# The matrix of one for the transposes: one counting instruction of GpSimd and one comparison, in place of a chain of pieces on VectorE

## Chip, cores and metric

One Trainium2 chip, one core. The time is device microseconds of one launch, the median of the timed runs. In rows of the trace PE is TensorE's matmul, PEld its weight load, DVE is VectorE, ACT ScalarE, POOL GpSimd, SP SyncE, which here does nothing but issue DMAs; a "q" behind the name is the engine's sequencer.

## What is computed

Block-causal attention (8 batches, 8 heads, 576 positions, 64 wide), then a gated feed-forward layer over all 4608 tokens:

```python
scores = q @ k.T / sqrt(64)            # (8, 8, 576, 576)
scores = where(pos_i // 64 >= pos_j // 64, scores, -1e9)
attn = softmax(scores) @ v             # heads side by side: x is (4608, 512)
g = x @ w_gate                         # (512, 1536)
out = (g / (1 + exp(-g)) * (x @ w_val)) @ w_out
```

The float64 weights are turned into pairs of float32 parts on the chip, so each product of the feed-forward layer is three matmuls (L1100 to L1102, L1191 to L1193).

## The kernel before

A planner in the kernel (`in_order`) simulates five engines with costs written by hand and lists all steps in one order; they are issued in that order, so every engine has a fixed queue. The planner's tasks begin behind the lines that the change touches, and neither its costs nor its ranks are touched.

Before the planner's list stands the setup. VectorE sets `ones`, `unseen` and `seen`. GpSimd clears tiles as they are made (the loop over `first_of`: `v` at L260, `ob` at L281, the key columns of `parts` at L234). Then VectorE makes `ident`, a 128x128 matrix with ones on its diagonal, in 13 instructions (L308 to L316): a row 0 to 127 by doubling, each partition's own number by a transpose and three additions, and one comparison.

`ident` is an operand of the transposes on TensorE (L411) that turn q and k of the first two batches. Those feed scores (L437), their maximum (VectorE L702, L705; GpSimd L709, a reduction over partitions), the subtraction (VectorE L733) and the exponential (ScalarE L737). The loads of q come by SyncE (L387), the first eight of k by ScalarE's queue (L387), v by SyncE (L754). In SyncE's queue the first load of `v0` is the third instruction, behind two loads of q; it waits for the GpSimd memset that clears `v0`. Behind it stand the loads of q for the second tile `qk1` and for the second half of `qk0`, and then the loads of the weights (L944).

Of the kernel before, what the change touches and what calls it, by code (L numbers as in the profile page):

```python
# [9 lines left out]
I32 = mybir.dt.int32  # L10
F16 = mybir.dt.float16
AF = mybir.ActivationFunctionType
ALU = mybir.AluOpType
# [5 lines left out]
def kernel(  # L19
# [17 lines left out]
    nc = tc.nc  # L37
# [3 lines left out]
    P = 128  # L41
# [64 lines left out]
    def pool_of(pool, tag, count, shapes=None, init=None, **variants):  # L106

        variants = variants or {"": (shapes, init)}
        kinds[tag] = pool, variants
        slots[tag] = [[None, None] for _ in range(count)]

    def tiles_of(tag, place, variant=""):
        pool, variants = kinds[tag]
        slot = slots[tag][place]
        if slot[0] != variant:
            shapes, init = variants[variant]  # L120
            names = [f"{tag}{place}_{k}" for k in range(len(shapes))]
            slot[:] = variant, [
                x and pool.tile(*x, name=name, tag=name, bufs=1) for x, name in zip(shapes, names)
            ]
            if init:
                init(*slot[1])
        return slot[1]
# [56 lines left out]
    ident = const.tile([P, P], F32, name="ident")  # L184
# [112 lines left out]
    pool_of(psum, "gv", 2, [([P, 2 * XT], F32)])  # L297
    pool_of(psum, "po", 1, [([P, 2, DM], F32)])

    first_of = [("v", ""), ("ob", "signs" if wide else "out"), ("parts", "pair"), ("xhl", ""), ("wo", "raw"), ("hhl", "")]  # L300
    for tag, variant in first_of:
        for place in range(len(slots[tag])):
            tiles_of(tag, place, variant)


    scratch = tiles_of("t", 0)[0]
    count, mine = scratch[:, 0:P], scratch[:, P : P + 32]
    nc.vector.memset(count[:, 0:1], 0.0)  # L308
    for i in range(7):
        n = 2**i  # L310
        nc.vector.tensor_scalar(count[:, n : 2 * n], count[:, 0:n], float(n), None, ALU.add)
    nc.vector.transpose(mine, count[:, 0:32])
    for i in range(1, P // 32):
        rows = slice(32 * i, 32 * (i + 1))
        nc.vector.tensor_scalar(mine[rows, 0:1], mine[rows, 0:1], 32.0 * i, None, ALU.add)
    nc.vector.tensor_scalar(ident, count, mine[:, 0:1], None, ALU.is_equal)  # L316

    x_d = dram.tile([DM, NT], F32, name="x_d")
    s_d = dram.tile([H, NT], F32, name="s_d")
# [1094 lines left out]
```

## Time and profile before

| | |
|---|---|
| median of 3 runs | 1178.03 us (1176.53 to 1178.63) |
| profiled execution | 1175.4 us |
| its span, first to last instruction | 1173.6 us |
| PE busy | 1145.5 us, 98% of the span |
| DVE, ACT, POOL busy | 758.9, 620.4, 325.5 us |

The span is what the trace covers; 1.8 us of the profiled execution lie outside it. A timeline row gives the start, how long it lasted, the engine, line and operation, and in brackets how long the engine sat idle before it and what released it.

### The profile page before, as it was taken

What the parts mean: (1) busy time and instruction counts of PE and PEld (TensorE: products, weight loads), DVE (VectorE), ACT (ScalarE), POOL (GpSimd) and SP (SyncE); (2) the same over time, 40 slices, a digit from 0 to 9 for tenths busy, and PEclk for the clock granted to TensorE, in tenths of its full rate; (3) what the DMA queues carried; (4) which work ended last, traced back from release to release, by engine and by line L of the source; (5) the groups of instructions that cost most, each with busy time, mean ns of one, the idle gap of its engine ahead of it and who ended that gap; (6) DMA issues with size and microseconds to landing.
All of it is one profiled execution on the core that took longest, in us unless ns stands there. A gap on an engine that the chain in (4) does not pass through costs nothing.

```text
span 1173.6 us, 21780 instructions
## 1 busy us (share of the span) xinstructions
PE 1145.5 (98%) x8512; PEld 1024.7 (87%) x8512; DVE 758.9 (65%) x1230; ACT 620.4 (53%) x1114; POOL 325.5 (28%) x139
## 2 busy tenths in 40 slices
PE   5889999999999999999999999999999999999998
PEld 4568778898898989988998899898989899999997
DVE  6988988575887668768575859575767533323222
ACT  6978876546573837465656555555646312212111
POOL 3222100144535251434444334252432500000000
PEclk9989999999999999999999999999999999999999
DMA  8658756766564756656565565655663445444432
GB/s 225 188 151 219 201 187 226 206 178 166 169 148 137 198 164 167 195 166 168 152 188 160 152 177 163 187 146 161 164 202 108 145 148 197 140 167 136 143 134 100
DMA packets 266982, 197.40 MB, mean 168 GB/s; under 512 B 195264, under 2 KB 231376, under 8 KB 266880
## 3 DMA queue, kind: packets, MB, share of 16 engines
q1 hardware_dynamic: 264304, 195.29, 56.9%
q8 instruction: 67, 1.10, 0.4%
q10 hardware_dynamic: 2576, 0.72, 0.3%
q14 instruction: 35, 0.29, 0.1%
HBM read 171.57 MB, written 24.38 MB: 167 GB/s over the span
## 4 chain that ended last, share of the span: by engine, by line
PE 85%; DVE 5%; ACT 4%; DMA 3%; issue 1%; POOL 1%; SPq 1%; ACTq 0%; DVEq 0%; POOLq 0%
PE gv L1100 16%; PE gv L1102 15%; PE gv L1101 15%; PE po L1191 7%; PE po L1193 7%; PE po L1192 7%; PE at L777 7%; PE at L564 6%; DVE sc L733 1%; DVE mx L705 1%; DMA wo<-in_moe_w_val_dram 1%; POOL mx L709 1%; DMA wo<-in_moe_w_out_dram 1%; ACT ob L959 1%; PE at L648 1%
## 5 line engine op out<-in xcount | busy, mean ns | idle before, releaser
L709 POOL PARTITION_ALL_REDUCE mx<-mx x80 | 144.1, 1850 | 408.7 <-issue 135.2
L1100 PE MATMUL gv<-xhl,v_all 128*128 128x256 f32 x864 | 241.8, 280 | 0.8 <-DVE t L1136 0.7
L1102 PE MATMUL gv<-xhl,v_all 128*128 128x256 f32 x864 | 239.7, 277 | 0.0
L1101 PE MATMUL gv<-xhl,v_all 128*128 128x256 f32 x864 | 239.3, 277 | 0.0
L828 POOL PARTITION_ALL_REDUCE mx<-mx x48 | 178.9, 3775 | 201.4 <-DVE mx L705 192.8
L1136 DVE SCALAR_TENSOR_TENSOR t<-t,gv 128x512 f32<-128x512 f32 x108 | 74.0, 685 | 215.4 <-ACT t L1133 215.2
L1100 PEld LDWEIGHTS gv<-xhl,v_all 128*128 128x128 f32 x864 | 162.1, 188 | 4.9 <-issue 2.5
L1101 PEld LDWEIGHTS gv<-xhl,v_all 128*128 128x128 f32 x864 | 162.3, 188 | 0.6
L1102 PEld LDWEIGHTS gv<-xhl,v_all 128*128 128x128 f32 x864 | 162.2, 188 | 0.2
L1133 ACT ACTIVATE t<-gv 128x512 f32<-128x512 f32 x108 | 64.6, 598 | 171.2 <-PE gv L1102 171.1
L1191 PE MATMUL po<-wo,hhl 128*128 128x512 f32 x372 | 147.7, 397 | 0.0
L1192 PE MATMUL po<-wo,hhl 128*128 128x512 f32 x372 | 145.6, 391 | 0.0
L1193 PE MATMUL po<-wo,hhl 128*128 128x512 f32 x372 | 145.1, 390 | 0.2 <-DVE hhl L1149 0.2
L1146 ACT CAST hhl<-t 128x512 fp32r<-128x512 f32 x108 | 67.0, 620 | 132.1 <-DVE t L1141 129.7
L733 DVE TENSOR_TENSOR sc<-sc,mx 128x640 f32<-128x640 f32 (+6 forms) x168 | 122.7, 765 | 11.7 <-POOL mx L709 11.6
L737 ACT ACTIVATE sc<-sc 128x1024 f32<-128x1024 f32 (+3 forms) x104 | 106.0, 1029 | 45.3 <-DVE sc L733 44.9
L1100 PE MATMUL gv<-xhl,g_even 128*128 128x256 f32 x432 | 123.7, 286 | 0.0
L1102 PE MATMUL gv<-xhl,g_even 128*128 128x256 f32 x432 | 122.2, 283 | 0.4 <-DVE g_even L981 0.4
L1101 PE MATMUL gv<-xhl,g_even 128*128 128x256 f32 x432 | 122.1, 283 | 0.0
L1100 PE MATMUL gv<-xhl,g_odd 128*128 128x256 f32 x432 | 120.7, 279 | 0.0
L1101 PE MATMUL gv<-xhl,g_odd 128*128 128x256 f32 x432 | 119.6, 277 | 0.0
L1102 PE MATMUL gv<-xhl,g_odd 128*128 128x256 f32 x432 | 119.6, 277 | 0.0
(171 smaller groups left out, 2368.8 us busy)
## 6 DMA issues: line engine op xcount, KB each, us to landing
wo<-wo_d SPq DMA_DIRECT2D x200, 512.0 KB
out_dram<-ob SPq DMA_DIRECT2D x35, 256.0 KB
v<-in_v_dram SPq DMA_DIRECT2D x64, 128.0 KB
xt<-x_d SPq DMA_DIRECT2D x64, 128.0 KB
rt<-r_d SPq DMA_DIRECT2D x128, 64.0 KB
qk<-in_q_dram SPq DMA_DIRECT2D x112, 72.0 KB
qk<-in_k_dram SPq DMA_DIRECT2D x104, 72.0 KB
x_d<-xu SPq DMA_DIRECT2D x24, 288.0 KB
```

What stands on the lines that cost most here:

```text
L709: nc.gpsimd.partition_all_reduce(m, m, channels=P, reduce_op=bass_isa.ReduceOp.max)
L733: nc.vector.tensor_tensor(piece(c), scores_of(c), m, ALU.subtract)
L737: nc.scalar.activation(x, x, AF.Exp)
L777: nc.tensor.matmul(ps[0][own(x), 1 - i if sums else i, q0 - s0 : s1 - s0], lhsT=ones if sums else vt[0][:, 2 * lane + c, own(x)], rhs=sc[0 ...
L828: nc.gpsimd.partition_all_reduce(m, m, channels=P, reduce_op=bass_isa.ReduceOp.add)
L1100: nc.tensor.matmul(o, lhsT=hi[:, d], rhs=xhi[:, 0:w], start=first, stop=False)
L1101: nc.tensor.matmul(o, lhsT=hi[:, d], rhs=xlo[:, 0:w], start=False, stop=False)
L1102: nc.tensor.matmul(o, lhsT=lo[:, d], rhs=xhi[:, 0:w], start=False, stop=last)
L1136: nc.vector.scalar_tensor_tensor(t[0][:, 0:n], t[0][:, 0:n], 1.0, pg[0][:, 0:n], ALU.add, ALU.mult)
L1191: nc.tensor.matmul(po, lhsT=hi, rhs=whi, start=i + y == 0, stop=False)
L1192: nc.tensor.matmul(po, lhsT=hi, rhs=wlo, start=False, stop=False)
L1193: nc.tensor.matmul(po, lhsT=lo, rhs=whi, start=False, stop=i + y == NFC - 1)
```

## The change

GpSimd's `iota` writes into each element of a scratch tile its column number minus its partition number, as int32; VectorE compares that with 0 and writes `ident`. This stands ahead of the `first_of` loop, so the iota is ahead of GpSimd's memsets, and the scratch tile `t0` is placed in memory ahead of the tiles of that loop.

```diff
+    scratch = tiles_of("t", 0)[0].bitcast(I32)[:, 0:P]
+    nc.gpsimd.iota(scratch, [[1, P]], channel_multiplier=-1)
+    nc.vector.tensor_scalar(ident, scratch, 0, None, ALU.is_equal)
+
     first_of = [("v", ""), ("ob", "signs" if wide else "out"), ("parts", "pair"), ("xhl", ""), ("wo", "raw"), ("hhl", "")]
     for tag, variant in first_of:
         for place in range(len(slots[tag])):
             tiles_of(tag, place, variant)
-
-
-    scratch = tiles_of("t", 0)[0]
-    count, mine = scratch[:, 0:P], scratch[:, P : P + 32]
-    nc.vector.memset(count[:, 0:1], 0.0)
-    for i in range(7):
-        n = 2**i
-        nc.vector.tensor_scalar(count[:, n : 2 * n], count[:, 0:n], float(n), None, ALU.add)
-    nc.vector.transpose(mine, count[:, 0:32])
-    for i in range(1, P // 32):
-        rows = slice(32 * i, 32 * (i + 1))
-        nc.vector.tensor_scalar(mine[rows, 0:1], mine[rows, 0:1], 32.0 * i, None, ALU.add)
-    nc.vector.tensor_scalar(ident, count, mine[:, 0:1], None, ALU.is_equal)
```

GpSimd's queue from the kernel's first instruction, before. The number at a tile's name is its place (`v0`, `v1`) and a running number; DVE_49 and Pool_49 are the semaphores that those engines count up.

```order
L260 MEMSET v0_0_78 128x640
L260 MEMSET v1_0_80 128x640
L281 MEMSET ob0_0_82 128x512
L281 MEMSET ob1_0_84 128x512
L234 MEMSET parts0_1_87 128x64
L234 MEMSET parts1_1_90 128x64
L709 ISA
L709 ISA mx0_0_181<-mx0_0_181 128x256 [waits DVE_49]
```

The same queue now (the lines move up by 8: L701 is what L709 was).

```order
L302 ISA
L302 IOTA t0_0_78 128x128
L260 MEMSET v0_0_81 128x640
L260 MEMSET v1_0_83 128x640
L281 MEMSET ob0_0_85 128x512
L281 MEMSET ob1_0_87 128x512
L234 MEMSET parts0_1_90 128x64
L234 MEMSET parts1_1_93 128x64
L701 ISA
L701 ISA mx0_0_170<-mx0_0_170 128x256 [waits DVE_49]
```

Two instructions came in at the front: the iota, and an ISA instruction without operands ahead of it, of the kind that already stood ahead of the first reduction over partitions and stands there still. All memsets moved behind both.

VectorE's queue before, from the transpose that makes the partitions' numbers to its first step of the planner's list (the doubling rows of L311 ahead of the transpose are not shown).

```order
L312 STREAM_TRANSPOSE t0_0_117<-t0_0_117 128x32
L311 TENSOR_SCALAR t0_0_117<-t0_0_117 128x64 [waits DVE_49]
L315 TENSOR_SCALAR t0_0_117<-t0_0_117 32x1 [waits DVE_49]
L315 TENSOR_SCALAR t0_0_117<-t0_0_117 32x1 x2
L316 TENSOR_SCALAR ident_63<-t0_0_117 128x128 [waits DVE_49]
L702 COPY mx0_0_181<-at0_0_171 128x2x128 [waits PE_49,Activation_49]
```

And now, from its setup memsets on.

```order
L190 MEMSET unseen_66 64x1
L192 MEMSET seen_69 128x1
L303 TENSOR_SCALAR ident_63<-t0_0_78 128x128 [waits Pool_49]
L694 COPY mx0_0_170<-at0_0_160 128x2x128 [waits PE_49,Activation_49]
L697 TENSOR_TENSOR mx0_0_170<-mx0_0_170,at0_0_160 128x2x128
```

Twelve instructions fewer stand there; the comparison that is left waits for GpSimd (Pool_49) in place of VectorE's own chain. SyncE's queue holds the same rows in the same order, its third row among them:

```order
L379 DMA qk0_0_126<-in_q_dram 96x3x64 x2
L746 DMA v0_0_81<-in_v_dram 128x2x64 [waits Pool_49]
L746 DMA v0_0_81<-in_v_dram 128x2x64
L379 DMA qk1_0_134<-in_q_dram 96x3x64 [waits DMAHW1_49]
L379 DMA qk1_0_134<-in_q_dram 96x3x64 [waits DMAHW3_49]
L379 DMA qk1_0_134<-in_q_dram 96x3x64 [waits DMAHW5_49]
L379 DMA qk1_0_134<-in_q_dram 96x3x64 [waits DMAHW7_49]
L379 DMA qk0_0_126<-in_q_dram 96x3x64 [waits DMAHW0_49]
```

Nothing moved here; the wait for Pool_49 is for the second thing that GpSimd finishes in place of the first.

## Rows read from the trace of the kernel before

**Rows 1.** The page: busy us, share of the span, instructions by engine.

```profile
PE 1145.5 (98%) x8512; PEld 1024.7 (87%) x8512; DVE 758.9 (65%) x1230; ACT 620.4 (53%) x1114; POOL 325.5 (28%) x139
```

**Rows 2.** Busy time by stretch: us, busy (instructions) by engine, PEclk, DMA share, GB/s.

```profile
core 0: us, PE busy (x) PEld busy (x) DVE busy (x) ACT busy (x) POOL busy (x), PEclk, DMA share, GB/s
0.00:10.00 10.00, 4.07 (x21) 3.05 (x21) 3.93 (x19) 3.45 (x7) 2.96 (x11) 1.00 0.77 178
...
30.00:40.00 10.00, 7.32 (x71) 5.18 (x67) 9.55 (x22) 9.40 (x18) 2.76 (x2) 1.00 0.66 162
...
60.00:66.10 6.10, 3.72 (x31) 2.47 (x29) 5.92 (x13) 5.00 (x11) 1.50 (x2) 1.00 0.24 52
66.10:72.90 6.80, 5.87 (x28) 3.04 (x30) 6.09 (x12) 3.47 (x8) 0.54 (x1) 0.50 0.75 209
...
100.00:120.00 20.00, 20.00 (x158) 16.81 (x157) 17.42 (x30) 18.16 (x36) 4.33 (x4) 1.00 0.92 262
```

**Rows 3.** Timeline of the first 20 us, engines mixed.

```profile
0.73 1.20 POOL L260 MEMSET v<- 128x640 f32 x2 [0.29 <-POOLq L1397]
...
1.69 0.97 SPq L754 DMA_DIRECT2D v<-in_v_dram  x2
...
2.85 0.23 POOL L234 MEMSET parts<- 128x64 f32 x2
2.98 3.77 SPq L387 DMA_DIRECT2D qk<-in_q_dram  x6
...
4.10 0.28 DVE L316 TENSOR_SCALAR ident<-t 128x128 f32<-128x128 f32 x1
...
4.44 1.22 PE L411 MATMUL gv<-ident,qk 96*128 96x96 f32 x6 [4.44 <-DVE ident L316]
5.37 0.74 ACT L419 ACTIVATE parts<-gv 128x288 f32<-128x288 f32 x2 [2.15 <-DMA qk<-in_k_dram]
...
8.74 0.42 DVE L702 COPY mx<-at 128x256 f32<-128x256 f32 x1 [4.36 <-ACT mx L482]
...
8.78 2.44 PE L411 MATMUL gv<-ident,qk 96*128 96x96 f32 x12 [0.97 <-DMA qk<-in_q_dram]
...
9.59 2.11 POOL L709 PARTITION_ALL_REDUCE mx<-mx  x2 [6.51 <-DVE mx L705]
...
11.73 1.02 DVE L733 TENSOR_TENSOR sc<-at,mx 128x512 f32<-128x512 f32 x2 [2.24 <-POOL mx L709]
...
14.76 0.85 ACT L737 ACTIVATE sc<-sc 128x768 f32<-128x768 f32 x1
```

**Rows 4.** Instructions of line L709: duration ns min/median/max, first and last start us.

```profile
L709 POOLq MODIFY_POOL_CONFIG  x2: 7/7/7, 3.1 to 3.1; - x2
```

**Rows 5.** Instructions of L260 and of L1244: duration ns min/median/max, first and last start.

```profile
L260 POOL MEMSET v<- x2: 632/632/632, 0.7 to 1.3; 128x640 f32 x2
L1244 ACT ACT_TABLE_LOAD  x1: 1283/1283/1283, 1.7 to 1.7; - x1
```

**Rows 6.** SyncE's queue, first 9 us: who waited for what, us in total, times, longest.

```profile
SPq L387 <- DMA qk<-in_k_dram: 0.8, 1, 0.8
...
SPq L387 <- DMA v<-in_v_dram: 0.5, 1, 0.5
```

**Rows 7.** Chain that ended last, first 9 us: start us, us, what.

```profile
3.15 2.76 DMA qk<-in_k_dram
...
5.93 0.31 SPq L387
...
6.29 2.36 DMA qk<-in_q_dram
```

**Rows 8.** Line L777 alone, two stretches with 40 matmuls each, columns as in Rows 2.

```profile
55.50:60.50 5.00, 4.33 (x40) 2.61 (x40) 1.00 0.49 142
66.90:74.40 7.50, 7.20 (x40) 3.79 (x40) 0.60 0.71 197
```

**Rows 9.** Tile `xhl` (8 buffers), 300 to 1170 us: duration ns min/median/max, first and last start.

```profile
L1101 PE MATMUL gv<-xhl,v_all x712: 276/276/283, 300.1 to 1164.0; 128*128 128x256 f32 x178
```

## The prediction

> **What bounds the kernel now.** I began with the page: PE is busy for 98% of the span [rows 1]. Then the busy time by stretch: from 100 us on PE has no gap (20.00 of 20.00 us), while in the first 10 us it is busy for 4.07, and around 30 to 40 us for 7.32, where DVE and ACT are at 9.55 and 9.40 of 10 [rows 2]. So the end is set by a full PE, and the start by how soon the first chain of load, transpose, scores, maximum and subtraction hands work to DVE and ACT. All five queues have a fixed order, and they need each other, so a delay of the first links moves everything behind them by as much; a gain counts only where the link is the last one.
>
> Is `ident` a last link? The timeline says that PE's first transposes wait 4.44 us for it [rows 3], which looks like a gain to be had. But what uses those transposes is ACT's L419 at 5.37, and its wait is for ACT's own queue of k loads [rows 3], and the chain that ended last does not run through `ident` at all: it goes from a load of k (3.15 to 5.91) to a load of q that SP issues at 5.93, a second one at 6.29 and its landing 2.36 us later, at 8.64, to PE's second transposes at 8.78 [rows 3, 7]. So the thing to watch at the start is SP's queue.
>
> **What is removed.** Twelve of 13 DVE instructions (L308 to L316), which ended at 4.10 + 0.28 = 4.38 us. DVE has nothing else to do until 8.74 [rows 3], so its time is worth nothing. Behind an earlier `ident` PE would transpose sooner, but ACT's two evacuations already run without a gap, 0.74 us from 5.37 on [rows 3], and ACT's own loads hold the first one there. Gain: 0.
>
> **What is added on VectorE.** One comparison, of the shape of the L316 that it replaces: 0.28 us [rows 3], after the iota.
>
> **What is added on GpSimd.** First the iota, 128 columns wide. It isn't in this trace. The memsets write 640 columns in 0.63 us [rows 5] and two of 64 in 0.23 [rows 3], a reduction of 256 columns takes about 1.05, half of the 2.11 for two [rows 3]. So it costs 0.1 to 1.05 us; I take 0.3, near the memsets, since it too writes without reading.
>
> Second, the ISA instruction without operands that now stands ahead of the iota, while the one ahead of the first reduction stays. In the trace the latter is two MODIFY_POOL_CONFIG records of 7 ns at 3.1 us [rows 4]. What it costs cannot be seen there: from 3.13 to 9.59 GpSimd has no record, and the reduction then starts as DVE's L705 releases it [rows 3]. So whatever the instruction set going took between nothing and 9.59 - 3.13 = 6.46 us, all of it hidden. This is the term that decides. I take it near the upper end, 6.46, for both: the only other row in which an engine fetches something before the first instruction of a kind is ACT's table load, with 1.28 us [rows 5], so nothing is unlikely, and the row of the same engine and the same instruction is the gap of 6.46. The other ends stay in the range. [...]
>
> **Who stands behind the iota.** GpSimd's memsets begin at 0.73 [rows 3]. With 6.46 + 0.3 ahead of them, `v0` is clear at 0.73 + 6.76 + 0.63 = 8.1 us, not at 1.36. SP's third instruction, the load of `v0`, waits for that; SP came to it at 1.69, so 1.69 - 1.36 = 0.3 us are covered. Behind it in SP's queue stand four loads of q for `qk1`, the two of q for `qk0` that are in the chain above, and the weights. Of the waits that SP has there now, the 0.5 us for v's landing moves along with v, but the 0.8 us for k's landing [rows 6] ends at 5.93 whatever SP does, and shrinks. Cover in all: 0.3 + 0.8 = 1.1 us. So the load that lands at 8.64 lands 6.76 - 1.1 = 5.7 us later, and with it PE's second transposes.
>
> **The other two paths.** `ident` is ready at 0.73 + 6.76 + 0.05 (semaphore) + 0.28 = 7.8, 3.4 us later than now: less than 5.7, so it isn't last. The second change of GpSimd starts behind the memsets, which take 0.73 to 3.08 now [rows 3]: 0.73 + 6.76 + 2.35 = 9.85, plus 6.46, so the first reduction can run at 16.3, not at 9.59. That is 6.7 us later, and DVE's first L733 with it: 18.4 to 19.4 in place of 11.73 to 12.75. What needs it, ACT's L737, ran at 14.76 [rows 3], 2.0 us behind L733's end, and moves to 20.5 by SP's delay, so the 6.7 are covered with 1.0 us to spare; DVE's steps on the weights squeezed in between may add 0.3. If the second change takes longer than about 7.5 us, this path is last instead.
>
> **Sum.** -0 + 5.7 = 5.7 us (6.0 with the squeeze). Against the profiled execution: 1175.4 + 5.7 = 1181.1, with a span of 1179.3. That run lies 2.6 us below the median, so for the median I forecast 1178.0 + 5.7 = **1183.7 us**. A measurement of this kernel can tell about 0.2%, 2.4 us, from no change.
>
> **Rivals.**
>
> 1. *The change of GpSimd's configuration is free, or nearly* (under 1.1 us each). For: two records of 7 ns, and SP's cover of 1.1 us swallows what there is; the iota's 0.3 us lies within it too. Against: it would have to be cheaper than ACT's table load. Time: 1178.0, since the gain is 0. This is also the case of the other side, not slower; it decides where the change plus the iota stay under 1.1 us.
>
> 2. *It costs, but less*: 1.3 us as ACT's table load, up to 5. Then 1.3 + 0.3 - 1.1 = 0.5 to 4.2 us: 1178.5 to 1182.2.
>
> 3. *It costs more*: the one ahead of the iota sets up something else than the old one, and the old one now runs among SP's held-back loads; 6.46 bounds only the old one where it stood. With 9 us each: 9.3 - 1.1 = 8.2 by SP; the reduction at 0.73 + 9.3 + 2.35 + 9 = 21.4, 11.8 later, of which the 2.0 us from L733's end at 12.75 to L737 cover some: 9.8. Time 1186.2 to 1187.8, and more above 9 us.
>
> [...]
>
> 5. *Addresses.* `t0` now lies ahead of `v0`, and all tiles of the loop move up by 2048 bytes. PE reads `xhl`, 8 buffers in a row, and 712 matmuls over all of them differ by 276 to 283 ns [rows 9]: no buffer is slower for where it lies. A nanosecond on each of 8512 matmuls would be 8.5 us, so the case keeps a small chance, either sign.
>
> **How the numbers follow.** Forecast with its own spread (each change 5.5 to 8 us: 1182.3 to 1186): 0.60. Rival 1: 0.13. Rival 2: 0.10. Rival 3: 0.08. Rivals 4 and 5 on their own: 0.09, half up, half down. The range 1178.0 to 1188.0 leaves out the lower half of rival 1, the top of rival 3 and the ends of 4 and 5, just under 0.2. Slower by over 2.4 us (above 1180.4): 0.60 + 0.08 + half of rival 2 (0.05) + 0.03 of rivals 4 and 5 = 0.76. Within: 0.13 + 0.05 of rivals 1 and 2, less 0.01 where rival 1 loses the dip too: 0.17. Faster: that and the rest of rivals 4 and 5: 0.07.
>
> **What would show it.** Right: GpSimd's iota starts near 7 us with no record ahead of it, its first memset of `v` behind it; SP's third instruction waits for GpSimd's memset at about 8; PE's first transposes at 7.9 and its second near 14.4; the first reduction at about 16, released not by DVE but by nothing the profile shows; from 20 us on the same rows as before, 5 to 6 us later. Rival 1 shows the iota below 1 us, `ident` near 1.4, and PE's first transposes waiting for loads. Rival 3 shows the reduction beyond 18. I would be wrong in the size if the shift at 20 us is there and has shrunk by 100 us, which would mean that DVE and ACT make up for a late start; and wrong in the mechanism if SP's `v0` load leaves at 1.7 as before.

## The result

1182.56 us, the median of 6 runs (1182.0 to 1184.09), beside 1178.33 for the kernel before (1176.44 to 1179.15): the ratio is 1.005, with a 95% interval of 1.004 to 1.006, so 4.7 to 7.1 us slower. The two medians alone lie 4.2 us apart, a little less than that. The forecast was 5.7 us more, and 1183.7 for the median. The profiled execution of the changed kernel took 1182.27 us, with this page line, which answers to [rows 1]:

```profile
PE 1149.5 (97%) x8512; PEld 1027.3 (87%) x8512; DVE 757.2 (64%) x1218; ACT 620.8 (53%) x1114; POOL 325.2 (28%) x140
```

VectorE's 12 instructions are gone (1230 to 1218) and its busy time is 1.7 us less; the span is 1180.5 us. What it looks like at the start is in the timeline of its first 28 us (columns as in [rows 3]):

```profile
7.94 0.23 POOL L302 IOTA t<- 128x128 int32 x1 [7.50 <-issue]
8.14 1.19 POOL L260 MEMSET v<- 128x640 f32 x2
8.21 2.31 DVE L303 TENSOR_SCALAR ident<-t 128x128 f32<-128x128 int32 x1 [7.07 <-POOL t L302]
8.78 0.92 SPq L746 DMA_DIRECT2D v<-in_v_dram  x2
...
10.21 0.23 POOL L234 MEMSET parts<- 128x64 f32 x2
...
10.58 1.22 PE L403 MATMUL gv<-ident,qk 96*128 96x96 f32 x6 [10.58 <-DVE ident L303]
...
14.51 2.44 PE L403 MATMUL gv<-ident,qk 96*128 96x96 f32 x12 [0.56 <-DMA qk<-in_q_dram]
...
15.22 0.41 DVE L697 TENSOR_TENSOR mx<-mx,at 128x256 f32<-128x256 f32 x1
...
16.41 2.15 POOL L701 PARTITION_ALL_REDUCE mx<-mx  x2 [5.98 <-DVE mx L697]
...
18.60 1.02 DVE L725 TENSOR_TENSOR sc<-at,mx 128x512 f32<-128x512 f32 x2 [2.96 <-POOL mx L701]
...
20.49 0.85 ACT L729 ACTIVATE sc<-sc 128x768 f32<-128x768 f32 x1
...
21.77 4.20 POOL L701 PARTITION_ALL_REDUCE mx<-mx  x4 [3.21 <-DVE mx L697]
```

GpSimd sits idle for 7.5 us ahead of the iota, "issue": nothing that the profile shows. The first reduction's row names VectorE's L697, but that had ended at 15.63, 0.78 us earlier; what ended last ahead of the reduction is the second change, 5.7 us behind its records at 10.7. The two records of the configuration change stand at 0.8 us, nearly as short as those of [rows 4]:

```profile
L302 POOLq MODIFY_POOL_CONFIG  x2: 11/11/11, 0.8 to 0.8; - x2
```

The chain that ended last, first 24 us, runs from that idle time through the memset of `v`, SP's queue and the load of q to PE's second transposes, where [rows 7] had ACT's and SP's loads from 3.15 on:

```profile
0.86 7.08 issue
7.94 0.23 POOL t L302
8.18 0.59 POOL v L260
...
9.23 2.02 DMA v<-in_v_dram
...
12.29 2.09 DMA qk<-in_q_dram
...
14.51 1.19 PE gv L403 x6
```

SP waited 0.8 and 0.5 us for landings in its first 9 us [rows 6]; now, in its first 13, it waits for none, and for GpSimd alone:

```profile
SPq L746 <- POOL v L260: 7.1, 1, 7.1
```

Against [rows 3], PE's first transposes are 6.1 us later, its second 5.7, the first reduction 6.8, L729 (L737 before) 5.7, and the second group of reductions 6.0, which before stood at

```profile
15.75 4.20 POOL L709 PARTITION_ALL_REDUCE mx<-mx  x4 [4.05 <-DVE mx L705]
```

From there it stays: PE is all but full from 100 us on (18.7 to 20.0 of every 20 us up to 180, and 18.9 to 20.0 in the kernel before), below as in [rows 2], and the last matmul of the row of [rows 9] starts at 1170.8 us in place of 1164.0.

```profile
0.00:10.00 10.00, 0.00 (x0) 0.00 (x0) 2.02 (x5) 1.49 (x2) 2.26 (x9) 1.00 0.34 76
...
100.00:120.00 20.00, 19.94 (x167) 16.05 (x165) 18.34 (x33) 18.21 (x37) 4.14 (x3) 1.00 0.85 234
```

The two profiled spans differ by 6.9 us, a little more than the 6.0 at 20 us. Between lie dips of the clock: one of 6.8 us at 0.50 in the kernel before [rows 2], two here in the first 100 us.

```profile
46.10:53.00 6.90, 5.08 (x22) 3.07 (x24) 6.89 (x15) 6.56 (x13) 0.00 (x0) 0.51 0.65 154
...
73.50:80.30 6.80, 5.92 (x28) 3.09 (x30) 5.77 (x11) 3.40 (x8) 0.86 (x1) 0.50 0.78 212
```

### The profile page after: what moved, and what is told of

Read it like the earlier page. It is cut to its first block, busy times and chain, and to the rows that moved or that the text cites. A ratio compares the mean times of both kernels' runs of the same rounds, so it can differ in the third digit from the quotient of the medians.

```text
span 1180.5 us, 21771 instructions
## 1 busy us (share of the span) xinstructions
PE 1149.5 (97%) x8512; PEld 1027.3 (87%) x8512; DVE 757.2 (64%) x1218; ACT 620.8 (53%) x1114; POOL 325.2 (28%) x140
## 4 chain that ended last, share of the span: by engine, by line
PE 88%; DVE 5%; ACT 3%; DMA 2%; issue 2%; POOL 1%; SPq 0%; DVEq 0%; POOLq 0%
PE gv L1092 16%; PE gv L1094 16%; PE gv L1093 16%; PE po L1183 7%; PE at L769 7%; PE po L1185 7%; PE po L1184 7%; PE at L556 6%; PE at L640 1%; DMA wo<-in_moe_w_out_dram 1%; PE at L429 1%; DVE mx L697 1%; DVE sc L725 1%; PE po L769 1%; DVE wo L965 1%
## 5 line engine op out<-in xcount | busy, mean ns | idle before, releaser
L701 POOL PARTITION_ALL_REDUCE mx<-mx x80 | 143.6, 1844 | 409.2 <-DVE mx L697 139.9
L729 ACT ACTIVATE sc<-sc 128x1024 f32<-128x1024 f32 (+3 forms) x104 | 105.9, 1028 | 45.7 <-DVE sc L725 45.4
```

The lines of the kernel that those rows point to most:

```text
L701: nc.gpsimd.partition_all_reduce(m, m, channels=P, reduce_op=bass_isa.ReduceOp.max)
L729: nc.scalar.activation(x, x, AF.Exp)
```

## Experiments

The theory after the result: GpSimd's change to the iota's configuration takes about 7 us (0.86 to 7.94) and holds its whole queue; the change back takes about 6 (10.7 to 16.41); and three paths wait for them (`ident`, SP's load of `v`, the first reduction), each about as late as the others. The rivals: one path carries the loss, or the tile's new place in memory does, or the comparison on int32. All times "over before" are from the ratio to the kernel before on the same chip, which took 1176 to 1177 us there.

**The iota behind the memsets** (SP's load of `v` is free, `ident` and the reduction are not).

```diff
     scratch = tiles_of("t", 0)[0].bitcast(I32)[:, 0:P]
-    nc.gpsimd.iota(scratch, [[1, P]], channel_multiplier=-1)
-    nc.vector.tensor_scalar(ident, scratch, 0, None, ALU.is_equal)
     first_of = [...]
     for tag, variant in first_of:
         ...
+    nc.gpsimd.iota(scratch, [[1, P]], channel_multiplier=-1)
+    nc.vector.tensor_scalar(ident, scratch, 0, None, ALU.is_equal)
```

> The iota, the configuration change ahead of it and the comparison stand behind GpSimd's memsets. If the comparison of the changed kernel took 2.31 us because GpSimd's memsets ran beside it: 0.28 us here, ident at 10.7, PE's first transposes at 10.8, second near 14.0, reduction at 16.5 to 17.5, time 4.5 to 6 us over before. If it took 2.31 us because its input is int32: 2.3 us again, PE's first transposes at 12.9, and 8 us over before.

1182.9 us, ratio 1.005 (1.0032 to 1.0068). From its timeline:

```profile
10.39 0.23 POOL L306 IOTA t<- 128x128 int32 x1 [7.36 <-issue]
10.66 0.23 DVE L307 TENSOR_SCALAR ident<-t 128x128 f32<-128x128 int32 x1 [9.52 <-POOL t L306]
10.94 1.22 PE L402 MATMUL gv<-ident,qk 96*128 96x96 f32 x6 [10.94 <-DMA v<-in_v_dram]
...
16.49 2.15 POOL L700 PARTITION_ALL_REDUCE mx<-mx  x2 [5.86 <-DVE mx L696]
```

The comparison takes 0.23 us with the same int32 input: the 2.31 us of the changed kernel were GpSimd's memsets beside it, which end at 10.44 there while the comparison ends at 10.52. And SP not being held gave nothing back: the other two paths are as late as they were.

**The kernel before, with `ident` by its 13 pieces, and an idle iota at the front** (SP and the reduction are held, `ident` is not).

```diff
+    spare = tiles_of("t", 0)[0].bitcast(I32)[:, 2 * P : 3 * P]
+    nc.gpsimd.iota(spare, [[1, P]], channel_multiplier=-1)
     first_of = [...]
```

> The 13 pieces of VectorE make ident as before; the iota stays at the front of GpSimd's queue and fills columns that nobody reads. If SP's load of v behind the late memset is a loss by itself: PE's first transposes at 4.4 or sooner, v loaded from 8.8, second transposes at 14.5, 5 to 5.7 us over before. If the late ident carries the loss: second transposes near 9, 0 to 1 us over before.

1182.47 us, ratio 1.0043 (1.0027 to 1.006), 3 to 7 us over before. `ident` is early, and the second transposes and the reduction are where they were:

```profile
4.04 1.20 PE L413 MATMUL gv<-ident,qk 96*128 96x96 f32 x6 [4.04 <-DMA qk<-in_q_dram]
...
14.77 2.44 PE L413 MATMUL gv<-ident,qk 96*128 96x96 f32 x12 [6.86 <-DMA qk<-in_q_dram]
...
16.50 2.15 POOL L711 PARTITION_ALL_REDUCE mx<-mx  x2 [6.04 <-issue]
```

**The same, the idle iota behind the memsets** (only the reduction is held).

```diff
     for tag, variant in first_of:
         ...
+    nc.gpsimd.iota(spare, [[1, P]], channel_multiplier=-1)
```

> As the one with the idle iota, but the iota stands behind the memsets, so that nothing but the first reduction waits for the two configuration changes. If the second change has to be waited for: iota near 10.2, reduction at 16.3 or so instead of 9.6, 4 to 5.5 us over before. If it is free or hidden: 0 us.

1184.09 us, ratio 1.0054 (1.0039 to 1.0069). PE's second transposes are nearly where they were before (9.62), but the reduction comes at 17.25, behind two configuration changes in a row, and L735 (L733 before) at 19.43 in place of 11.73:

```profile
9.62 2.44 PE L413 MATMUL gv<-ident,qk 96*128 96x96 f32 x12 [1.37 <-DMA qk<-in_q_dram]
...
10.84 0.23 POOL L306 IOTA t<- 128x128 int32 x1 [7.76 <-issue]
...
17.25 2.15 POOL L711 PARTITION_ALL_REDUCE mx<-mx  x2 [6.17 <-issue]
19.43 1.02 DVE L735 TENSOR_TENSOR sc<-at,mx 128x512 f32<-128x512 f32 x2 [9.50 <-POOL mx L711]
```

So the reduction's path alone is enough for the whole loss (4.6 to 8.1 us over before), and the two experiments before this one show that freeing SP's load or `ident` by itself gives nothing back. Neither of these two was held alone.

**The memsets on VectorE.**

```diff
     scratch = tiles_of("t", 0)[0].bitcast(I32)[:, 0:P]
     nc.gpsimd.iota(scratch, [[1, P]], channel_multiplier=-1)
-    nc.vector.tensor_scalar(ident, scratch, 0, None, ALU.is_equal)
     first_of = [...]                      # v, ob and parts cleared by nc.vector.memset
     for tag, variant in first_of:
         ...
+    nc.vector.tensor_scalar(ident, scratch, 0, None, ALU.is_equal)
```

> The changed kernel with the memsets of v, ob and parts on VectorE ahead of the comparison. Comparison 0.28 us if the memsets of GpSimd were what it waited for, 2.3 us if int32 is. With 0.28: ident at 8.5, PE's first transposes at 8.6, SP not held, reduction free to run near 14.3, about 4 us over before. With 2.3 us: 6 us over before.

1180.52 us, ratio 1.0031 (1.002 to 1.0042), 2.4 to 4.9 us over before.

```profile
8.43 0.23 POOL L302 IOTA t<- 128x128 int32 x1 [7.99 <-issue]
8.70 0.23 DVE L307 TENSOR_SCALAR ident<-t 128x128 f32<-128x128 int32 x1 [4.98 <-POOL t L302]
...
14.73 2.15 POOL L700 PARTITION_ALL_REDUCE mx<-mx  x2 [6.06 <-DVE mx L696]
```

With nothing of GpSimd's behind the iota, the second change starts 1.8 us sooner (behind the iota's end at 8.66, in place of the memsets' at 10.44), the comparison finds GpSimd quiet, and SP loads `v` from 1.84 on. Part of the loss is saved so, while both changes are still paid; one of the ten executions, at 6448.8 us, isn't in the ratio.

**The configuration change first, then the memsets, then the iota.** `load_library` writes the ISA row of the queue by hand.

```diff
-    nc.gpsimd.iota(scratch, [[1, P]], channel_multiplier=-1)
-    nc.vector.tensor_scalar(ident, scratch, 0, None, ALU.is_equal)
+    nc.gpsimd.load_library(library_config.standard)
     first_of = [...]
     for tag, variant in first_of:
         ...
+    nc.gpsimd.iota(scratch, [[1, P]], channel_multiplier=-1)
+    nc.vector.tensor_scalar(ident, scratch, 0, None, ALU.is_equal)
```

> The configuration change stands first in GpSimd's queue, then the memsets, then the iota and the comparison. If the change holds the whole queue: memsets from 7.9 us, iota near 10.2, ident at 10.6, 5 to 6 us over before. If it holds only instructions that need it: memsets from 0.75, v loaded from 1.7, iota at 7.9, ident at 8.4, reduction near 14, 4 us over before.

1184.78 us, ratio 1.0063 (1.0039 to 1.0087), 4.6 to 10.2 us over before. The memset waits, though memsets ran before any change in the kernel before:

```profile
8.94 1.19 POOL L260 MEMSET v<- 128x640 f32 x2 [8.50 <-issue]
...
11.21 0.23 POOL L307 IOTA t<- 128x128 int32 x1
```

So the change holds the whole queue, not only the instructions that need it.

**Two more changes at the front.**

```diff
+    nc.gpsimd.load_library(library_config.standard)
+    nc.gpsimd.load_library(library_config.all_libraries[1])   # the reduction's
     nc.gpsimd.iota(scratch, [[1, P]], channel_multiplier=-1)
```

> The changed kernel with two more configuration changes at the front (to the reduction's and back). If each costs what the rows of the changed kernel show, 5.7 to 7.1 us, and nothing hides it: iota at 20 to 22, and 12 to 14 us over the changed kernel, 1194 to 1197. If a change is cheap and something else held the iota: within 2 us of the changed kernel.

1197.11 us, ratio 1.0172 (1.0138 to 1.0206): 20 us over before, 14.5 over the changed kernel's median. The records of the three lines say what each takes, since each waits for the one ahead:

```profile
L302 POOLq MODIFY_POOL_CONFIG  x2: 11/11/11, 0.8 to 0.8; - x2
L303 POOLq MODIFY_POOL_CONFIG  x2: 7/7/7, 8.3 to 8.4; - x2
L304 POOLq MODIFY_POOL_CONFIG  x2: 7/7/7, 13.9 to 14.0; - x2
L304 POOL IOTA t<- x1: 233/233/233, 21.7 to 21.7; 128x128 int32 x1
```

To the iota's configuration 7.5 us (0.8 to 8.3) and 7.7 (14.0 to 21.7), to the reduction's 5.5 (8.4 to 13.9), and a shift of the start passes on to the end in full.

**The new place of `t0` alone.** The kernel before, with `t0` placed ahead of the other tiles.

```diff
+    tiles_of("t", 0)
     first_of = [...]
```

> The kernel before, with its t0 placed in memory ahead of the tiles of the loop, as in the changed kernel, and nothing else. If places don't matter: within 1 us of before and the same durations for the matmuls over xhl, 276 ns. If they do: a nanosecond on each matmul is 8.5 us, either way.

1175.83 us, ratio 0.9999 (0.9986 to 1.0012), and the matmuls of [rows 9] last 276 ns as before. Places don't matter here.

**One change in place of two.** VectorE fills `ident` with ones, and GpSimd's `affine_select`, for which the change to the reduction's configuration is enough (below it starts at 3.21, right behind the memsets), clears all but the diagonal.

```diff
-    nc.gpsimd.iota(scratch, [[1, P]], channel_multiplier=-1)
-    nc.vector.tensor_scalar(ident, scratch, 0, None, ALU.is_equal)
+    nc.vector.memset(ident, 1.0)
+    nc.gpsimd.load_library(library_config.all_libraries[1])   # the reduction's
     first_of = [...]
     for tag, variant in first_of:
         ...
+    nc.gpsimd.affine_select(ident, ident, [[1, P]], ALU.is_equal, 0.0, base=0, channel_multiplier=-1)
```

> VectorE fills ident with ones, GpSimd clears all but the diagonal with one affine_select, which comes with the reduction's configuration, so there is one change, at the front of GpSimd's queue, and none ahead of the reduction. If the change holds the whole queue: ident near 10, 4.5 to 5.7 us over before, reduction released by VectorE. If it doesn't hold the memsets: ident near 7.7, 3 to 4 us over before.

1176.18 us, ratio 0.9991 (0.9979 to 1.0003): as before, against both expectations. The change at the front, with its records at 0.9 us, took 0.2 us at most: GpSimd sat idle for 0.45 us ahead of the first memset, against 0.29 in the kernel before [rows 3].

```profile
0.96 1.20 POOL L260 MEMSET v<- 128x640 f32 x2 [0.45 <-POOLq L1389]
...
3.21 0.29 POOL L308 TENSOR_SCALAR_AFFINE_SELECT ident<-ident 128x128 f32<-128x128 f32 x1
```

This made a new theory: a change is free when the configuration is already in place, and the last execution of the same kernel left it in place. The next three tell it from "the reduction's change is cheap by itself".

**One change, with the other configuration left behind at the end.**

```diff
     for t in order:
         t.fn()
+    nc.gpsimd.load_library(library_config.standard)
```

> The kernel with one affine_select and one change at the front, and behind its last reduction the change to the iota's configuration. If its front change was free because the configuration was in place from the execution before: now it takes 5.4 to 6.2 us, memsets from 6.5, ident near 9, second transposes near 13, 4 to 5 us over before. If that change is cheap by itself: as without the addition, 0 us.

1181.7 us, ratio 1.0042 (1.0028 to 1.0056). The same front, and now it costs 5.8 us, from the records at 1.1 to the first memset:

```profile
L303 POOLq MODIFY_POOL_CONFIG  x2: 11/11/11, 1.0 to 1.1; - x2
```

```profile
6.94 1.19 POOL L260 MEMSET v<- 128x640 f32 x2 [6.44 <-issue]
```

**The changed kernel, with the iota's configuration left behind at the end.** The same line behind its last reduction.

> The changed kernel, and behind its last reduction, where GpSimd has nothing left to do, one more configuration change, to the iota's. If a change to what is in place already is free, also from one execution to the next: the change ahead of the iota costs nothing, iota near 1.0, v loaded from 2, ident by 3.4 (its comparison beside the memsets), the reduction's change from 3.4 to 9.2, just hidden; time within 0.2% of before. If a change costs its 7 us each time: iota at 8 again and 5 to 6 us over before.

1176.74 us, ratio 0.9997 (0.9986 to 1.0007): the whole loss is gone, with the iota still at the front.

```profile
1.08 0.24 POOL L302 IOTA t<- 128x128 int32 x1 [0.64 <-POOLq L1390]
1.27 1.28 POOL L260 MEMSET v<- 128x640 f32 x2
1.35 0.63 DVE L303 TENSOR_SCALAR ident<-t 128x128 f32<-128x128 int32 x1 [0.22 <-POOL t L302]
...
9.87 2.15 POOL L701 PARTITION_ALL_REDUCE mx<-mx  x2 [6.22 <-DVE mx L697]
```

The added change stands at 939 us, where GpSimd has nothing left to do. `ident` is ready at 2.0 us in place of 4.4, and the time is that of the kernel before.

**The kernel before, with the iota's configuration left behind.** The same line.

> The kernel before, with the same change behind its last reduction, so that the one ahead of its first reduction can't find its configuration in place. At 5.4 to 6.2 us from 3.13 it ends between 8.5 and 9.3, and the reduction at 9.6 still hides it: within 0.2% of before, reduction released by VectorE near 9.6. If it takes over 6.5 us: reduction later than 9.6, up to 1 us over before.

1176.28 us, ratio 1.0006 (0.9995 to 1.0016): the time is that of the kernel before, but the reduction is not where it was. Before, it started 0.09 us behind the end of VectorE's L705, at 9.59 [rows 3]:

```profile
9.09 0.41 DVE L705 TENSOR_TENSOR mx<-mx,at 128x256 f32<-128x256 f32 x1
```

Here it starts 0.45 us behind that end, at 9.98:

```profile
9.12 0.41 DVE L705 TENSOR_TENSOR mx<-mx,at 128x256 f32<-128x256 f32 x1
...
9.98 2.15 POOL L709 PARTITION_ALL_REDUCE mx<-mx  x2 [6.91 <-DVE mx L705]
```

The row names VectorE, but the change most likely ended last: 6.91 us behind GpSimd's memsets, which is the most that it can have taken, nearly all of it hidden. The 0.4 us that it comes later cost nothing that the medians show.

No version beats the kernel before; four equal it (the places, the one change, and the two kernels with the iota's configuration left behind).

## Why the prediction was right, and where it was not

**The sum.** SP's path was foreseen 5.7 us late at PE's second transposes, and it was: 14.51 against 8.78. The squeeze of VectorE was foreseen with 0.3 on top, and the second group of reductions is 6.0 us late. The first reduction was foreseen at 16.3 and came at 16.41; ACT's exponential at 20.5, and it came at 20.49. A late start passes on to the end, as the three changes show, where 13.8 us at the iota (21.70 against 7.94) became 14.5 at the end.

**The price of a change.** The step that failed is the price read off GpSimd's gap between 3.13 and 9.59: "between nothing and 9.59 - 3.13 = 6.46 us, all of it hidden", of which the prediction took the upper end for both changes. In the kernel before it most likely took next to nothing: it changes to the configuration that the execution before had left in place, as the front change of the kernel with one change does (0.96 against 6.94 where another was left). The first two reductions bear this out: together they take 2.11 us in the kernel before [rows 3] and with one change, and 2.15 in each of the ten kernels in which their configuration had to be changed to first. So the gap bounded nothing. The size came out near by luck: to the iota's 7.1 us in the changed kernel (0.86 to 7.94) and 7.1 to 8.1 in the others, to the reduction's 5.5 to 5.9, and 6.9 at most in the kernel before with the iota's left behind, where both were taken as 6.46.

In the sum two errors cancel: the memset of `v` is 7.4 us late (8.14 against 0.73), not 6.76, but what SP made up was 1.7, not 1.1. Its load of `v` is 7.1 late; the waits for landings behind it [rows 6] are gone, that for `v` too, so the load of q is issued 6.0 late (12.29 against 6.29); and it landed in 2.09 us in place of 2.36 [rows 7].

**`ident`.** It was foreseen at 7.8 and came at 10.52: the comparison was priced at 0.28 us by the row of the kernel before, in which no memset ran beside it (the 0.05 us for the hand-over, an estimate, was near: the iota ends at 8.17, the comparison starts at 8.21). Beside six memsets it took 2.31 us, behind them 0.23. The row that could have said so was in the trace of the kernel before: six of the seven additions of L311, up to 32 columns wide, last 2.16 us in all beside the same memsets, and 1.19 where no memset runs, in the kernel with the idle iota at the front.

```profile
1.20 2.16 DVE L311 TENSOR_SCALAR t<-t 128x1 f32<-128x1 f32 x6
```

```profile
1.20 1.19 DVE L312 TENSOR_SCALAR t<-t 128x1 f32<-128x1 f32 x6
```

No row says what holds the comparison: it starts at 8.21, 0.07 us behind the first memset, and ends at 10.52, 0.08 behind the last. The error did no harm to the sum, because the other two paths were as late: with `ident` early and the idle iota at the front, the time was the same.

**Rivals.** Free (1): false for the changed kernel, true where a configuration is in place. Cheaper (2): false. Dearer (3): false in size, but its reason holds, since the change ahead of the iota is another one and takes longer than the reduction's (7.1 to 8.1 us against 5.5 to 5.9). Addresses (5): false by the places alone (ratio 0.9999). Dips of the clock (4, which has its share in the chances): no run shows what a dip adds to the time. What they show is one dip in the first 100 us of the kernel before and two in the changed kernel, with a mean granted clock of 0.996 and 0.994 in the profiled executions; the other eleven kernels, of either kind, had 0.991 to 0.996 there, and the four that equal the kernel before had 0.991 to 0.994. Whether the start shifts the dips these runs don't tell. The 6.0 us at 21.77 are there ahead of the first dip of the changed kernel, at 46.1.

**What is removed.** That `ident` is no last link was right: in the kernel with the configuration left behind it comes 2.4 us sooner, for nothing.

## What to carry to other kernels

An instruction of GpSimd that needs another configuration than its neighbours cost here not its own 0.23 us but two changes, of about 7 and 6 us, and the time of everything queued behind them; look in the order for the ISA rows without operands, not in the trace, where they were 7 to 11 ns long at the start of these kernels. An idle stretch that hides a cost says nothing about that cost: it may be zero, and may be zero only because the execution before left things in place. The rows fit executions that each follow one of the same kernel (the iota at 1.08 us where that one leaves its configuration, at 7.94 where not); none shows what another kernel in between would leave. Where three paths are late by nearly the same, taking one out of the way gives nothing back; remove what they share.

## What the runs showed of the hardware

- A GpSimd configuration change holds the whole queue, memsets too, for 5.5 to 5.9 us (the reduction's, in one kernel up to 6.9) or 7.1 to 8.1 (the iota's), with two records of 7 to 11 ns at the start of the kernel and of 88 at its idle end; the rest is idle time, which the profile puts down to "issue" or to another engine that had ended earlier. Why the two differ is open.
- It took next to nothing (0.96 against 6.94 for the first memset, which starts at 0.73 with no change ahead of it; 1.08 against 7.94 for the iota) when the execution before had left the configuration in place.
- A VectorE comparison of 128x128, of int32, takes 0.23 us alone and 2.31 beside a row of GpSimd memsets, until the last of them is over (10.52 against 10.44); in the changed kernel with the configuration left behind it took 0.63 and ended at 1.98, with the memsets running to 3.65. Why it differs is open.
